# Where a layer's last projection and its early row maxima run: four transformer layers in fp32 on one core

## The chip, the core and the metric

One Trainium2 chip, one of its cores. The time is that of one execution of the whole program on the device, in microseconds (us); lower is better. TensorE (PE) multiplies matrices into the eight banks of its accumulator memory, VectorE (DVE) and ScalarE (ACT) read those banks, GpSimd (POOL) works on the other memory, and SyncE (SP) issues the transfers.

## The reference

Four layers, A, B, A, B, each of the form x = x + attention(layernorm(x)). x has 2048 rows of 576 numbers; there are 32 heads of 18.

```python
def _A_ref(x, wqkv, wo):            # every head has its own keys and values
    qkv = (x @ wqkv).reshape(B, S, 3, H, Dh).transpose(2, 0, 3, 1, 4)
    q, k, v = qkv[0], qkv[1], qkv[2]
    p = softmax(einsum("bhqd,bhkd->bhqk", q, k) * Dh ** -0.5)
    return einsum("bhqk,bhkd->bhqd", p, v).transpose(0, 2, 1, 3).reshape(B, S, D) @ wo
# _B_ref is the same, with one head of keys and values that all 32 heads of queries share
x = x + _A_ref(_layernorm(x), A_wqkv, A_wo)
x = x + _B_ref(_layernorm(x), B_wq, B_wk, B_wv, B_wo)
x = x + _A_ref(_layernorm(x), A_wqkv, A_wo)
x = x + _B_ref(_layernorm(x), B_wq, B_wk, B_wv, B_wo)
```

## The kernel before

**Units.** A layer's attention is cut into 64 units: 16 pairs of heads (a = 0 and 1, on the upper and the lower half of TensorE's rows) by 4 blocks of 512 queries. A unit has 32 score matmuls for row maxima (queries on the partitions, 128x512, read by DVE, which reduces each to its maximum), 32 score matmuls for the exponentials (keys on the partitions, 128x512, read by ACT, which writes `pt` or `side`), and the products of exponentials and values (PV), 16 chunks of 256 columns, summed in the bank `oacc`. The maxima of a unit must be known before its exponentials, since they go into the score matmul as two more rows of `big` (by way of DVE's transpose `tr`, the tensor `m_d` and a transfer). So maxima run 14 steps (`LEAD`) ahead, 56 of them before the first unit.

**Order inside a unit.** The order is written by hand: `UNIT` lists 24 entries, each with two letters, one for each a (`e` exponential, `m` maximum, `d` and `t` the two halves of a cheaper way to take two maxima: ACT writes a difference to `side`, DVE then adds it to a score and takes the maximum in one instruction; a star means that one instruction reads two neighbouring banks), and the PV columns that follow the entry. `BANKS` says which of the seven banks of `banks` each entry takes. PV trails by `LAG` = 1152 columns, so that the first unit's entries 1 to 9 have no PV behind them; `oacc` is idle there. The first two units' maxima don't use `d` and `t` (`FIRST_SHARED`): the buffer `side` lies where the transposed input `xx` lies, and is handed out when the projections are through.

**The head of a layer.** Before the units a layer is normalised, transposed and projected: `project(T, t)` is 14 matmuls of 512 columns ("terms" below: high and low parts of the weights `big` by those of the input `xx` or `yx`) into one bank, which ACT and DVE (or, with `filler`, ACT twice and then POOL) split into a high and a low part, stored to `qk_d` and loaded from there into `big` by `load_k` and `load_q`. `project_v_part` is 14 matmuls of 288 columns for the values. Into this work `beat` weaves the 56 maxima, four at a time (one call of `max_pairs`; the calls are numbered 1 to 14 here): `woven(f, left, every)` calls f `left` times, each after `every` terms. In A layers all 14 calls lie in the list `fill` (eight `project_v_part`, then four projections). In B layers five calls lie among the projections of the third block of tokens (T = 2), five among those of the fourth (T = 3), where `project(3, 4)` makes the keys, and four in `fill` (two projections). A call's four maxima take the banks 4, 5, 6 and one of 0 to 3, which the projections take in turn too. In B layers calls 10 and 11 read the keys of the fourth block.

**Queues.** Each engine works strictly in the order of the code. SP waits for each transfer's inputs in order too, so a load behind a store waits for the store's turn.

Of the kernel before, what the change touches and what calls it, by code (L numbers as in the profile page):

```python
# [9 lines left out]
F32 = mybir.dt.float32  # L10
# [9 lines left out]
P = 128  # L20
# [25 lines left out]
STEPS = 8  # L46
LEAD = 14

FREE = 8, 4
NM_AT = 3  # L50
ROW_AT = 5
SUM_AT = 4
# [77 lines left out]
ENDS = ends(UNIT[:CUT_AT])  # L130
MAX_OPS = [max_ops(k[CUT:] + k[:CUT]) for k in KINDS]
PLAIN = [(i // 2 % 4, i // 8 % 2 * 2 + i % 2) for i in range(16)]
FIRST_SHARED = 2


class Engine:
# [78 lines left out]
def tile_kernel(ctx: ExitStack, tc: tile.TileContext, A_x, A_wqkv, A_wo, B_x, B_wq, B_wk, B_wv, B_wo, out):  # L215
# [58 lines left out]


    turns = {"e": [0, 1, 2, 3], "m": [4, 5, 6]}

    def bank(b, name=None):
        return banks[:, b]
# [263 lines left out]
    for layer in range(4):  # L543
# [9 lines left out]


        def project(T, t, filler=False, half=None, terms=TERMS):
            t0 = T * 512
            n = 114 if not is_a and t == 4 else P
            ps = half_done.pop(t) if t in half_done else (etile if filler else mtile)("psq")
            us = slice(0, 2) if half is None else slice(half, half + 1)
            w = wtile(t)  # L560
            for xc, wc in terms:
                pe.matmul(ps[:n].rearrange("p (u t) -> p u t", u=2)[:, us], w[:, wc, :n], xts[T][:, us, xc, :],
                       start=(xc, wc) == TERMS[0], stop=(xc, wc) == (TERMS if half != 0 else TERMS_LO)[-1])
                beat()
            if half == 0:
                half_done[t] = ps
                return
            ev = [ptile("ev", dt=F32R) for _ in range(2)]
            ev_f = [e.bitcast(F32) for e in ev]
            act.activation(ev[0][:n], ps[:n], AF.Copy)  # L570
            r0, r1 = ((64, P) if t == 4 else (0, P)) if is_a else (96, 96 + DH)
            if T < 2 and t in (range(4, 9) if is_a else (4,)):
                key_diff(T, t, ps, r0, r1)
            if filler:
                raw = ptile("raw")
                act.activation(raw[:n], ps[:n], AF.Copy)
                nc.gpsimd.tensor_tensor(ev[1][:n], raw[:n], ev_f[0][:n], op=OP.subtract)
            else:
                dve.tensor_tensor(ev[1][:n], ps[:n], ev_f[0][:n], op=OP.subtract)
            if not is_a and t == 4:  # L580
                vt = ptile("t")
                act.activation(vt[64:82], ps[64:82], AF.Copy)
                store(ev_f, 96, 96 + DH, D, t0)
                store(ev_f, 0, 64, 512, t0)
                vts.append((T, vt))
            elif t == 4:
                store(ev_f, 64, P, D, t0)
                store(ev_f, 0, 64, 512, t0)
            else:
                store(ev_f, 0, P, t * P, t0)  # L590
# [165 lines left out]
            for a in range(2):  # L756
                max_mm(a, functools.partial(bank, b + a), joined)

        kept = []

        def max_pair():
            if is_a and m_done[0] % 4 == 0:
                run_todo(m_done[0] // 4)
            for a in range(2):
                if m_done[0] % 4 < 3:
                    max_mm(a, mtile)
                else:
                    max_mm(a, (lambda name: kept.pop(0)) if kept else etile)
            if not is_a and m_done[0] == 46:
                max_store(0, 0)  # L770
            elif not is_a and m_done[0] == 50:
                max_rows(0, 0)
# [63 lines left out]
        for T in range(4):  # L836
# [6 lines left out]
                ts = (4, 0, 1, 2, 3) if T < 3 else (4, 0, 1)  # L843
            for i, t in enumerate(ts):
                if not is_a and T == 2 and i == 1:
                    woven(max_pairs, 5, 10)
                elif not is_a and T == 3:
                    woven(max_pairs, *((1, 7), (2, 6), (2, 6))[i])
                project(T, t, not is_a and T >= 2)
                if is_a and T == 3 and i == 2:  # L850
                    load_k(0, 0, 1536)
# [63 lines left out]
        def pts_of(p, u, kc):  # L915

            if (p, u, kc) not in pts:
                n_p[0] += 1
                r = n_p[0] // 3 % 3
                if n_p[0] % 3 or (p, u) == (NPAIR - 1, 3) or sided.get(r) in pts:  # L920
                    pts[p, u, kc] = two("pt")
                else:
                    pts[p, u, kc] = side[:, 3 + 2 * r:5 + 2 * r]
                    sided[r] = p, u, kc
# [87 lines left out]
        for p in range(NPAIR):  # L1012
# [8 lines left out]
                for i in range(4 if is_a else 2):  # L1021
                    at(LEAD + 32 * (p - 1) + 1 + 8 * i if p else LEAD + 6 + i, load_part, p + 1, i)
            if is_a or p == 0:
                at(max(LEAD + 32 * (p - 2) + 20, LEAD + 10 * p), load_kd, p)
        for c in range(5):
            at(49 + 4 * c, finish_loads)
            at(48 + 4 * c, load_wsm, c, A_wo if is_a else B_wo, nc.gpsimd, nc.gpsimd, True)
# [15 lines left out]
        at(b - 2, out_t, 0, dve)  # L1043
        at(b - 1, out_rows, 1)
        left = LEAD - m_done[0] // 4
        work = len(TERMS) * sum(288 / 512 if f is project_v_part else 1 for f, _ in fill)
        woven(max_pairs, left, (work - FREE[layer % 2]) / left)
        for f, args in fill[:-1]:
            f(*args)
        kept.extend([etile("psm") for _ in range(weave["left"])])  # L1050
        fill[-1][0](*fill[-1][1])
        assert not weave["left"] and not kept
        halves.clear()
        side = xtile("side", (P, 9, 512), F32)
        late, n_r, n_p, sided = LAG, [0], [0], {}
        for w in range(4 * NPAIR):
            p, u = divmod(w, 4)
            more_m = w < 4 * NPAIR - 2
# [2 lines left out]
            for i, (kinds, cols) in enumerate(table):  # L1061
# [17 lines left out]
                            max_mm(a, take)  # L1079
                skip = min(late, cols)  # L1080
                late -= skip
                pv_cols(cols - skip)
            assert e_next == [16, 16]
        assert not diffs[0] and not diffs[1]
        outs = out_proj(layer == 3)
        for st in range(ns, ns + L_AT + 1):
# [37 lines left out]
```

## Time and profile before

| | |
|---|---|
| median of 3 runs | 5536.77 us (5536.75 to 5538.99) |
| the profiled execution | 5534.68 us, of which its span 5532.5 us |
| PE, DVE, ACT, POOL busy | 99%, 89%, 85%, 26% of the span |
| mean granted clock of TensorE | 0.998 |

The span runs from the first to the last instruction; some 2.2 us lie around it. The first unit of the four layers begins at about 211, 1537, 2967 and 4297 us. Matmuls are pipelined and their ends are modelled, so waits of PE are read from the distances between the starts of its rows.

### The profile page before, as it was taken

How to read it: one execution, taken by the hardware profiler on the slowest of the kernel's cores; microseconds unless marked ns; L12 is line 12 of the kernel's file. 1: busy time of each engine (PE TensorE's matmuls, PEld its weight loads, DVE VectorE, ACT ScalarE, POOL GpSimd, SP SyncE). 2: the span in 40 equal slices, each digit the busy share in tenths (PEclk: the TensorE clock that was granted, in tenths of full speed). 3: DMA queues.
4: the chain of work that ended last, by engine and by line, in shares of the span. 5: the costliest groups of instructions: out<-in, count | busy, mean ns of one | idle time of the engine just before them, and what ended most of it. 6: DMA issues, size and time to landing. Idle time of an engine off the chain costs nothing.

```text
span 5532.5 us, 163956 instructions
## 1 busy us (share of the span) xinstructions
PE 5494.3 (99%) x63772; PEld 3242.2 (59%) x63772; DVE 4936.3 (89%) x9004; ACT 4709.4 (85%) x7780; POOL 1424.3 (26%) x3267
## 2 busy tenths in 40 slices
PE   9999999999999999999999999999999999999999
PEld 8655555555855555555686555555558555555556
DVE  5799999997699999999647999999977999999995
ACT  3599999999289999999625999999992999999995
POOL 3132222223232222222321322222232322222221
PEclk9999999999999999999999999999999999999999
DMA  7321111111421110101253211111114211110102
GB/s 241 110 50 37 41 37 41 38 37 34 130 63 25 24 25 21 25 22 25 62 202 94 51 40 37 41 37 41 35 36 135 55 25 25 25 25 21 25 15 81
DMA packets 295540, 295.34 MB, mean 53 GB/s; under 512 B 151132, under 2 KB 228188, under 8 KB 285040
## 3 DMA queue, kind: packets, MB, share of 16 engines
q1 hardware_dynamic: 294760, 284.85, 18.3%
q8 instruction: 500, 8.19, 0.6%
q14 instruction: 280, 2.29, 0.1%
HBM read 158.77 MB, written 121.95 MB: 51 GB/s over the span
## 4 chain that ended last, share of the span: by engine, by line
PE 96%; DVE 1%; ACT 1%; issue 0%; SPq 0%; DMA 0%; POOL 0%; ACTq 0%; DVEq 0%; POOLq 0%
PE banks L147 58%; PE oacc L147 38%; DVE mx L147 1%; ACT pt L147 0%; ACT side L147 0%; DMA qk_d<-ev 0%; DVE yx L147 0%; DVE xx L147 0%; DVE xh L147 0%; SPq L977 0%; ACT raw L147 0%; ACT ev L147 0%; DVE ev L147 0%; SPq L1000 0%; DVE st L147 0%
## 5 line engine op out<-in xcount | busy, mean ns | idle before, releaser
L147 DVE TENSOR_REDUCE mxd<-banks 128x1 f32<-128x512 f32 (+1 forms) x6200 | 3955.6, 705 | 143.5 <-PE banks L147 112.6
L147 ACT ACTIVATE pt<-banks 128x512 f32<-128x512 f32 (+1 forms) x4248 | 2927.9, 740 | 120.5 <-PE banks L147 83.3
L147 PE MATMUL banks<-big 62*128 62x512 f32 (+1 forms) x15640 | 2784.9, 438 | 13.8 <-DVE mx L147 4.6
L147 PEld LDWEIGHTS banks<-big 62*128 62x128 f32 (+1 forms) x15640 | 1571.9, 184 | 1158.1 <-DVE mxd L147 538.0
L147 ACT ACTIVATE side<-banks 128x512 f32<-128x512 f32 (+1 forms) x2836 | 1907.2, 697 | 66.0 <-PE banks L147 65.6
L147 PE MATMUL oacc<-pt,vbuf 128*19 128x256 f32 (+3 forms) x20496 | 1279.7, 342 | 0.0
L981 POOL TENSOR_TENSOR rl<-lt,mone 128x8 f32<-128x8 f32 x256 | 428.3, 1673 | 1339.9 <-DMA lt<-os 1298.3
L147 PEld LDWEIGHTS oacc<-pt,vbuf 128*19 128x19 f32 x20496 | 450.6, 98 | 505.1 <-issue 329.7
L147 PE MATMUL oacc<-side,vbuf 128*19 128x256 f32 (+3 forms) x10064 | 676.9, 341 | 2.3 <-DVE ocv L147 2.3
L893 POOL TENSOR_TENSOR tree<-mxd 128x16 f32<-128x16 f32 x248 | 53.1, 214 | 1860.3 <-DVE mxd L147 1860.3
L147 DVE CUSTOM_DVE_ANT_0 side<-banks,side 128x512 f32<-128x512 f32 x744 | 499.0, 671 | 1.3 <-PE banks L147 1.0
L147 PE MATMUL oacc<-pt,vy 128*19 128x256 f32 (+3 forms) x8176 | 444.1, 312 | 0.0
L147 PEld LDWEIGHTS oacc<-side,vbuf 128*19 128x19 f32 x10064 | 223.3, 98 | 246.6 <-issue 157.2
L147 ACT ACTIVATE ev<-banks 128x512 fp32r<-128x512 f32 (+1 forms) x112 | 66.9, 598 | 321.6 <-PE banks L147 245.3
L147 PEld LDWEIGHTS oacc<-pt,vy 128*19 128x19 f32 x8176 | 190.5, 98 | 179.7 <-issue 115.3
L147 PE MATMUL banks<-kd,big 54*128 54x512 f32 x744 | 295.2, 397 | 0.0
L147 PE MATMUL banks<-wsm,ot 128*128 128x288 f32 x1792 | 243.7, 296 | 2.1 <-issue 2.1
L147 PEld LDWEIGHTS banks<-wsm,ot 128*128 128x128 f32 x1792 | 238.4, 188 | 6.4 <-issue 5.2
L147 PE MATMUL oacc<-side,vy 128*19 128x256 f32 (+3 forms) x4016 | 240.7, 311 | 0.0
L147 DVE TENSOR_TENSOR ev<-banks,ev 128x512 fp32r<-128x512 f32 (+1 forms) x84 | 57.9, 690 | 171.6 <-ACT ev L147 156.3
L147 PE MATMUL banks<-xx,big 128*128 128x512 f32 (+1 forms) x784 | 195.3, 398 | 4.1 <-ACT raw L147 4.1
L147 PE MATMUL banks<-yx,big 128*128 128x512 f32 (+2 forms) x812 | 193.8, 391 | 4.4 <-DVE yx L147 2.5
(91 smaller groups left out, 2690.4 us busy)
## 6 DMA issues: line engine op xcount, KB each, us to landing
big<-qk_d SPq DMA_DIRECT2D x180, 432.0 KB
qk_d<-ev SPq DMA_DIRECT2D x96, 512.0 KB
qk_d<-ev SPq DMA_DIRECT2D x120, 256.0 KB
rb<-r_d SPq DMA_DIRECT2D x1024, 18.0 KB
o_d<-os SPq DMA_DIRECT2D x1024, 18.0 KB
lt<-os SPq DMA_DIRECT2D x1024, 1.0 KB
o<-o_d SPq DMA_DIRECT2D x64, 256.0 KB
big<-m_d SPq DMA_DIRECT2D x512, 4.0 KB
```

Of the source, the lines that this page charges most:

```text
L147: i = f(*args, **kw)
L893: nc.gpsimd.tensor_tensor(above, mx[:, :, 0:2], mx[:, :, 2:4], op=OP.subtract)
L981: nc.gpsimd.tensor_tensor(rl, lts.pop((p, u)), mone, op=OP.pow)
```

## The change

The last projection of `fill` is taken out of the head. Its 14 terms run in the first unit, 7 behind entry 3 and 7 behind entry 6, into `oacc`, which PV doesn't need yet; ACT reads it out behind the second seven. `side` is handed out only after that, so the third chunk of exponentials goes to an ordinary `pt` buffer, and the third unit's maxima too are taken without `d` and `t` (`FIRST_SHARED` 3). The maxima of the head no longer take banks in turn: each pair goes to banks 3 and 4 or to 5 and 6, by turns, and one DVE instruction reduces both banks; the projections beside them keep banks 0 to 2. The calls come at other distances: in A layers every 7.36 terms' worth in place of 7.93; in B layers six among T = 2 (every 9 terms, before five, every 10), six among T = 3 (before five), two in `fill` (before four). The transfer `load_kd` of the first pair moves half a unit later.

```diff
-FREE = 8, 4
+FREE = 2, 2
-FIRST_SHARED = 2
+FIRST_SHARED = 3
+FIRST_FILL = 7, 7
+    max_banks = [3, 5]
         def project(T, t, filler=False, half=None, terms=TERMS):
+            for _ in project_terms(T, t, filler, half, terms):
+                beat()
+
+        def project_terms(T, t, filler=False, half=None, terms=TERMS, ps=None):
-            ps = half_done.pop(t) if t in half_done else (etile if filler else mtile)("psq")
+            if ps is None:
+                ps = half_done.pop(t) if t in half_done else (etile if filler else mtile)("psq")
-                beat()
+                yield
         def max_pair():
-            for a in range(2):
-                if m_done[0] % 4 < 3:
-                    max_mm(a, mtile)
-                else:
-                    max_mm(a, (lambda name: kept.pop(0)) if kept else etile)
+            b = max_banks.pop(0)
+            max_banks.append(b)
+            max_two(b)
                 if not is_a and T == 2 and i == 1:
-                    woven(max_pairs, 5, 10)
+                    turns["e"].remove(3)
+                    woven(max_pairs, 6, 9)
                 elif not is_a and T == 3:
-                    woven(max_pairs, *((1, 7), (2, 6), (2, 6))[i])
+                    woven(max_pairs, *((2, 6), (2, 6.5), (2, 6.5))[i])
-                if n_p[0] % 3 or (p, u) == (NPAIR - 1, 3) or sided.get(r) in pts:
+                if n_p[0] % 3 or side is None or (p, u) == (NPAIR - 1, 3) or sided.get(r) in pts:
-                at(max(LEAD + 32 * (p - 2) + 20, LEAD + 10 * p), load_kd, p)
+                at(max(LEAD + 32 * (p - 2) + 20, LEAD + 10 * p, LEAD + 4), load_kd, p)
+        last_terms = project_terms(*fill.pop()[1], ps=oacc)
+        if is_a:
+            turns["e"].remove(3)
         woven(max_pairs, left, (work - FREE[layer % 2]) / left)
-        for f, args in fill[:-1]:
+        for f, args in fill:
             f(*args)
-        kept.extend([etile("psm") for _ in range(weave["left"])])
-        fill[-1][0](*fill[-1][1])
-        side = xtile("side", (P, 9, 512), F32)
+        side, first_fill = None, list(FIRST_FILL)
                 skip = min(late, cols)
                 late -= skip
+                if skip and first_fill:
+                    for _ in range(first_fill.pop(0)):
+                        next(last_terms)
+                    if not first_fill:
+                        assert next(last_terms, True)
+                        side = xtile("side", (P, 9, 512), F32)
                 pv_cols(cols - skip)
```

PE's order at the end of the first layer's head, before: `xx,big` rows are terms, `big` rows with x4 are a call's maxima, the x24 are the first unit's entries 1 to 12 (row 83 is the end of the last projection), `oacc<-pt` is the first PV.

```order
79 L147 MATMUL banks<-xx,big 128x512 x8
80 L147 MATMUL banks<-big 128x512 x4
81 L147 MATMUL banks<-xx,big 128x512 x8
82 L147 MATMUL banks<-big 128x512 x4
83 L147 MATMUL banks<-xx,big 128x512 x7
84 L147 MATMUL banks<-big 128x512 x24
85 L147 MATMUL oacc<-pt,vbuf 19x256 x4
```

The same place of the changed kernel:

```order
79 L148 MATMUL banks<-xx,big 128x512 x7
80 L148 MATMUL banks<-big 128x512 x4
81 L148 MATMUL banks<-xx,big 128x512 x7
82 L148 MATMUL banks<-big 128x512 x4
83 L148 MATMUL banks<-xx,big 128x512 x2
84 L148 MATMUL banks<-big 128x512 x6
85 L148 MATMUL oacc<-xx,big 128x512 x7
86 L148 MATMUL banks<-big 128x512 x6
87 L148 MATMUL oacc<-xx,big 128x512 x7
88 L148 MATMUL banks<-big 128x512 x12
89 L148 MATMUL oacc<-pt,vbuf 19x256 x4
```

Two terms, not seven, lie between call 14 (row 82) and the first unit, and the last projection stands in two sevens between its entries.

PE's order in a B layer's fourth block, before: row 2465 is the second half of the key projection `project(3, 4)` (114 columns of weights), the `big` rows are calls 7, 8, 9 and 10, `ident,t` turns the values.

```order
2465 L147 MATMUL banks<-xx,big 114x512 x7
2466 L147 MATMUL banks<-xx,big 128x512 x6
2467 L147 MATMUL banks<-big 128x512 x4
2468 L147 MATMUL banks<-xx,big 128x512 x6
2469 L147 MATMUL banks<-big 128x512 x4
2470 L147 MATMUL banks<-xx,big 128x512 x2
2471 L147 MATMUL banks<-ident,t 128x18 x4
2472 L147 MATMUL banks<-xx,big 128x512 x6
2473 L147 MATMUL banks<-big 128x512 x4
2474 L147 MATMUL banks<-xx,big 128x512 x6
2475 L147 MATMUL banks<-big 128x512 x4
2476 L147 MATMUL banks<-xx,big 128x512 x8
```

And in the changed kernel, where the `big` rows are calls 8, 9 and 10:

```order
2466 L148 MATMUL banks<-xx,big 114x512 x6
2467 L148 MATMUL banks<-big 128x512 x4
2468 L148 MATMUL banks<-xx,big 114x512 x2
2469 L148 MATMUL banks<-xx,big 128x512 x7
2470 L148 MATMUL banks<-big 128x512 x4
2471 L148 MATMUL banks<-xx,big 128x512 x6
2472 L148 MATMUL banks<-big 128x512 x4
2473 L148 MATMUL banks<-xx,big 128x512
2474 L148 MATMUL banks<-ident,t 128x18 x4
```

Between the end of the key projection and call 10, the first that reads those keys, stood 26 terms, three calls and the turning of the values; now there are 13 terms and one call.

## Rows read from the trace of the kernel before

**Rows 1.** Page, part 4: the chain that ended last, by engine, then by line.
```profile
PE 96%; DVE 1%; ACT 1%; issue 0%; SPq 0%; DMA 0%; POOL 0%; ACTq 0%; DVEq 0%; POOLq 0%
```

**Rows 2.** Timeline, DVE: start, us, instruction; one transpose a unit, each in a unit's middle.
```profile
220.40 0.20 DVE L147 STREAM_TRANSPOSE tr<-hl 128x32 f32<-128x32 f32 x1
238.75 0.20 DVE L147 STREAM_TRANSPOSE tr<-hl 128x32 f32<-128x32 f32 x1
...
1548.14 0.20 DVE L147 STREAM_TRANSPOSE tr<-hl 128x32 f32<-128x32 f32 x1
...
2978.94 0.20 DVE L147 STREAM_TRANSPOSE tr<-hl 128x32 f32<-128x32 f32 x1
2998.42 0.20 DVE L147 STREAM_TRANSPOSE tr<-hl 128x32 f32<-128x32 f32 x1
...
4306.70 0.20 DVE L147 STREAM_TRANSPOSE tr<-hl 128x32 f32<-128x32 f32 x1
```

**Rows 3.** Timeline, PE, first layer's head and first unit; brackets: idle before, who ended it.
```profile
168.27 2.13 PE L147 MATMUL banks<-wsm,xx 128*128 128x288 f32 x15
...
171.00 2.14 PE L147 MATMUL banks<-wsm,xx 128*128 128x288 f32 x14
173.07 0.73 PE L147 MATMUL banks<-big 62*128 62x512 f32 x4
173.73 2.11 PE L147 MATMUL banks<-wsm,xx 128*128 128x288 f32 x14
...
207.49 0.73 PE L147 MATMUL banks<-big 62*128 62x512 f32 x4
...
211.28 0.97 PE L147 MATMUL banks<-big 64*128 64x512 f32 x6 [0.80 <-ACT raw L147]
...
216.98 0.85 PE L147 MATMUL oacc<-pt,vbuf 128*19 128x256 f32 x16
```

**Rows 4.** Windows of all engines: PE, PEld, DVE, ACT, POOL busy, granted clock, DMA.
```profile
2969.50:2976.00 6.50, 6.09 (x33) 3.38 (x33) 5.92 (x10) 4.96 (x8) 1.76 (x8) 0.50 0.57 163
1540.00:1545.50 5.50, 5.50 (x31) 2.82 (x32) 4.66 (x8) 4.08 (x8) 1.76 (x8) 0.50 0.54 153
```

**Rows 5.** Timeline, PE: first exponentials of the second and third layers.
```profile
1537.22 0.97 PE L147 MATMUL banks<-big 64*128 64x512 f32 x6 [0.81 <-ACT raw L147]
...
2967.43 1.78 PE L147 MATMUL banks<-big 62*128 62x512 f32 x9 [1.24 <-ACT raw L147]
```

**Rows 6.** Lines with shapes kept apart, DVE: instructions, busy us, mean ns, idle before.
```profile
L147 DVE TENSOR_REDUCE mxd<-banks 128x1 f32<-128x512 f32 x5952 | 3695.8, 683 | 143.5 <-PE banks L147 112.6
...
L147 DVE TENSOR_REDUCE mxd<-banks 128x2 f32<-128x1024 f32 x248 | 301.7, 1217 | 0.0
```

**Rows 7.** Timeline, DVE: the four maxima of the call at 173.07.
```profile
173.60 2.48 DVE L147 TENSOR_REDUCE mx<-banks 128x1 f32<-128x512 f32 x4 [0.24 <-PE banks L147]
```

**Rows 8.** Timeline, PE, fourth layer: key projection's end, calls 7 and 10, first unit.
```profile
4270.85 3.24 PE L147 MATMUL banks<-xx,big 128*114 128x512 f32 x13
4274.02 0.73 PE L147 MATMUL banks<-big 62*128 62x512 f32 x4
...
4282.69 0.73 PE L147 MATMUL banks<-big 62*128 62x512 f32 x4
...
4297.02 1.78 PE L147 MATMUL banks<-big 62*128 62x512 f32 x9 [1.24 <-ACT raw L147]
...
4303.23 0.85 PE L147 MATMUL oacc<-pt,vbuf 128*19 128x256 f32 x16
```

**Rows 9.** Timeline, SP, fourth layer: the keys' load (x2), a store, the load behind it.
```profile
4276.93 1.23 SPq L670 DMA_DIRECT2D big<-qk_d  x2
...
4280.20 0.35 SPq L625 DMA_DIRECT2D qk_d<-ev  x1
4283.21 0.65 SPq L670 DMA_DIRECT2D big<-qk_d  x2
```

**Rows 10.** Timeline, ACT, first layer: the first of the last projection's two readings.
```profile
210.14 0.60 ACT L147 ACTIVATE ev<-banks 128x512 fp32r<-128x512 f32 x1 [4.51 <-PE banks L147]
```

More of the change, by code (lines that the diff above doesn't have):

```diff
@@ L757, in max_two @@
                 max_mm(a, functools.partial(bank, b + a), joined)
-        kept = []
         def max_pair():
@@ L1045, in tile_kernel @@
         left = LEAD - m_done[0] // 4
+        last_terms = project_terms(*fill.pop()[1], ps=oacc)
         work = len(TERMS) * sum(288 / 512 if f is project_v_part else 1 for f, _ in fill)
+        if is_a:
+            turns["e"].remove(3)
         woven(max_pairs, left, (work - FREE[layer % 2]) / left)
-        for f, args in fill[:-1]:
+        for f, args in fill:
             f(*args)
-        kept.extend([etile("psm") for _ in range(weave["left"])])
-        fill[-1][0](*fill[-1][1])
-        assert not weave["left"] and not kept
-        halves.clear()
-        side = xtile("side", (P, 9, 512), F32)
+        assert not weave["left"]
         late, n_r, n_p, sided = LAG, [0], [0], {}
+        side, first_fill = None, list(FIRST_FILL)
         for w in range(4 * NPAIR):
@@ L1081, in tile_kernel @@
                 late -= skip
+                if skip and first_fill:
[4 more added lines that the diff above has]
+                        side = xtile("side", (P, 9, 512), F32)
                 pv_cols(cols - skip)
             assert e_next == [16, 16]
+        turns["e"].append(3)
         assert not diffs[0] and not diffs[1]
```

## The prediction

> **What bounds the kernel now.** I read the page's chain first: 96% of it is TensorE's work [rows 1], so the kernel is as long as PE's matmuls and PE's pauses. Next, DVE's one transpose a unit shows the pace: 18.35 us a unit [rows 2]. The order of instructions is the same from the third unit of each layer on; only four heads and the units behind them can change. I therefore went to PE's timeline there, with what DVE, ACT and SP do beside it.
>
> The prices come from two places. In the first layer 14 value terms take 2.07 us (171.00 to 173.07) and a call's four maxima 0.66 (to 173.73) [rows 3]; in the fourth 13 terms of 512 columns take 3.17 [rows 8]. A call is two pairs of matmuls, each pair side by side on the halves of the array. With t for a 512-column term or pair and s for each change between whole and half rows, 13t + s = 3.17 and 2t + s = 0.66: t = 0.228, s = 0.20, and a value term is 0.133. The calls of the first layer's head come 2.7 apart, which is 14 x 0.133 + 0.20 + 0.66: PE is full there. It pauses at the head's end, where it waits for ACT's reading, and in the first unit, where 12 pairs (2.7 us) take 5.70, from 211.28 to 216.98 [rows 3]. There DVE and ACT set the pace, PE has some 2.8 us to spare, and it is there that the change puts 3.2 us of terms.
>
> **The clock.** In the second and third layers the granted clock is 0.50, the lower of its two levels (1.2 of 2.4 GHz), for a stretch of the first unit [rows 4]; before the fall PE had only short pauses, 0.81 and 1.24 us [rows 5]. From the first exponential to the unit's middle the four layers take 9.12, 10.92, 11.51 and 9.68 us [rows 2, 3, 5, 8]; the third layer's next unit takes 19.48 instead of 18.35. So the low clock costs 1.2 in the second layer (against the fourth, a B layer too) and 2.4 + 1.1 in the third: 4.8 in all. With 14 more matmuls in just this stretch I expect no fall there: **-4.8** (0 if the falls stay).
>
> **A heads.** One reduction of two banks shows 1217 ns, a single one 683 [rows 6], and four singles take 2.48, so one each 0.60 [rows 7]; the double one then costs 0.60 + 0.53 = 1.13, a call 2.26 of DVE in place of 2.39. But fixed banks make a call wait for the last. DVE starts 0.53 behind PE (173.07 to 173.60) [rows 3, 7]; its second reduction starts at 1.66 and ends at 2.88, and only then can PE write banks 5 and 6. Spaced by work alone, calls 13 value terms apart come every 2.59; with T and T' two calls, the pair on 5 and 6 starts no sooner than T + 2.94, and the spacing settles at half of 2.94 + 0.43 plus the terms between: 2.65, and 2.59 for 7 terms (2.46 by work). Thirteen spacings (seven of 13 value terms, the rest 7, 8 or 11 terms mixed) sum to 34.3, so call 14 starts at 168.27 + 2.07 + 34.3 = 204.6; now it is 207.49. Behind it stand two terms, then entry 1, which takes the bank of the third projection: PE waits for ACT's two readings, 1.14 from the start of the first to PE's restart (210.14 to 211.28) [rows 3, 10]. That puts the first exponential at 204.6 + 2.6 = 207.2, 4.1 sooner.
>
> **The first unit.** Twelve pairs, 14 terms and four more changes of rows are 2.7 + 3.2 + 0.8 = 6.7 us of PE. On top, ACT reads the projection twice (1.1) in front of entry 7's exponential; entries 10 and 12 want banks that ACT frees late, and PE waits about 1.4, and 0.3 at entry 2 for bank 6. The first PV comes 8.5 behind the first exponential, not 5.7. Bounds: 5.7, if the terms fit in the gaps, to 5.7 + 3.2 + 0.8 + 1.1 = 10.8; I take 8.5, for PE's order is fixed and the gaps are not where the terms stand. First PV: 207.2 + 8.5 = 215.7 against 216.98: **-1.2 in each A layer**.
>
> **B heads.** Here DVE has the transposed input's low parts to make as well, and one more call stands before T = 3. Worked call by call with the same rule, the waits for banks 3 to 6 grow by about 1.7 us up to the key projection's end, and two more calls precede it (2 x 0.86): it ends at 4275.8; now at 4270.85 + 7 x 0.228 = 4272.4 [rows 8]. The keys then go through ACT, POOL and two transfers. Their loads leave SP from 4276.93 to 4278.16; a store in that queue holds its reader until 2.66 after its issue (4280.55 to 4283.21) [rows 9], so they land near 4281, and at the latest at 4282.69, where call 10 reads them without a pause [rows 8]. From projection to landed keys it is thus 5.8 to 10.3; I take 8.9, near the store's. Now 10.3 us of other work lie between. After the change there are 13 terms, one call and two changes, 4.0: **PE waits 4.9 for the keys** (1.8 to 6.3), behind it stand all the terms and calls 11 to 14, and DVE runs dry. Call 10 starts at 4284.7, 2.0 later than now. From there 29 terms, five calls and their changes, the values' turning, bank waits of 1.8 and ACT's reading make 14.4 to the first exponential (4299.1, now 4297.02), and 8.5 to the first PV: 4307.6 against 4303.23, **+4.4 in each B layer**.
>
> **Third unit's maxima, SP and POOL.** Three `d`/`t` pairs become six plain maxima: DVE pays three more of 0.60, 1.8 a layer, and ACT loses three readings. A unit's 24 single maxima, one double and three pairs (no less than three singles) hold DVE 17.3 of 18.35, so two units have 2 us of room: 0 to 1.8 a layer, taken as **+0.3**, x4. The moved projection's store now stands behind the next pair's first load, whose reader is more than half a unit away; `load_kd` and the later `side` are read a unit later: nothing. The row of maxima that the first exponential needs is ready sooner by as much as the calls are.
>
> **Sum.** -4.8 - 2 x 1.2 + 2 x 4.4 + 4 x 0.3 = +2.8 us. The profiled execution had 5534.68 (span 5532.5 and 2.2 around it) and becomes 5537.5; the median of the runs is 2.1 above it, so the forecast is **5539**.
>
> **Rivals.** *The clock falls in the B heads.* The wait for the keys is four times the longest pause ahead of a fall now. If the clock falls there, PE's work between call 10 and the first exponential (29 terms and five calls, 11 us) runs in part at half speed. By the falls seen a fall costs 1.2 to 3.5; if the low level lasts the whole way, 11. At 6 a layer the sum is +14.8: 5551, slower. It decides above 4 a layer. The Trainium skill speaks for it ("TensorE: Matmul & The Clock Gate", section "HAM oscillation — how this bites in real kernels"): a pause of PE on a transfer throttles the clock, so that the next matmuls start slow. The trace agrees that pauses bring a fall, but its falls followed pauses of about 1 us, so no row here shows what a long one does. *The terms do fit.* If the first unit's start takes 6.5 in place of 8.5 (DVE and ACT had work in hand when the terms begin), that is -2.0 x 4; if the keys land 5.8 behind the projection, the wait is 1.8, another -3.1 x 2. Sum: 2.8 - 8 - 6.2 = -11.4: 5525, faster. For it speaks that PE idles half of this stretch today; against it that the keys' path has five steps in strict order. *The low clock stays in the middle layers*: +4.8, 5544, no change that shows.
>
> **How the numbers follow.** 0.2% is 11 us, about what a measurement of this kernel can tell from no change. The forecast with its own bounds (5530 to 5547; the third rival in it) has 0.59, the faster rival 0.22, the slower 0.19. The range, 5523 to 5551, reaches to both, and leaves out only their far ends: the terms for nothing and a low clock over a whole head.
>
> **What will show it.** PE's rows in A heads: calls 2.6 apart, first PV 8 to 9 us behind the first exponential. In B heads: at call 10 a pause of some 5 us that the profile puts down to the transfer `big<-qk_d`, first PV some 23 us behind call 10 (now 20.5). In the windows: granted clock 1.00 at the first units, and whether it is 0.50 behind call 10. The prediction is wrong if the keys' pause is under 2 us, or if the first unit costs no more than now.

## The result and the profile after

The changed kernel takes 5546.25 us, the median of 20 runs (5543.62 to 5550.42); the kernel before, run beside it, takes 5535.85 (20 runs). The ratio is 1.0019 [1.0013, 1.0026]: 10.4 us slower, 7 above the forecast and inside its range. One execution each of two versions below took far longer (19179 us for e6_a_shared2, the profiled one; 6346 us for e8_order_shared2) and is left out. The profiled execution's span grew by 9.7, from 5532.5 to 5542.2 us. On the page almost nothing moves; the chain that ended last is again PE's.

```profile
PE 96%; DVE 1%; ACT 1%; issue 1%; DMA 0%; POOL 0%; SPq 0%; POOLq 0%; ACTq 0%; DVEq 0%
```

DVE's timeline after, one transpose a unit, answers to [rows 2]: the first three of the first layer, then the second and third of the other layers.

```profile
197.10 0.20 DVE L148 STREAM_TRANSPOSE tr<-hl 128x32 f32<-128x32 f32 x1
...
220.23 0.20 DVE L148 STREAM_TRANSPOSE tr<-hl 128x32 f32<-128x32 f32 x1
239.48 0.20 DVE L148 STREAM_TRANSPOSE tr<-hl 128x32 f32<-128x32 f32 x1
...
1553.45 0.20 DVE L148 STREAM_TRANSPOSE tr<-hl 128x32 f32<-128x32 f32 x1
1572.68 0.20 DVE L148 STREAM_TRANSPOSE tr<-hl 128x32 f32<-128x32 f32 x1
...
2982.00 0.20 DVE L148 STREAM_TRANSPOSE tr<-hl 128x32 f32<-128x32 f32 x1
3001.24 0.20 DVE L148 STREAM_TRANSPOSE tr<-hl 128x32 f32<-128x32 f32 x1
...
4316.26 0.20 DVE L148 STREAM_TRANSPOSE tr<-hl 128x32 f32<-128x32 f32 x1
4335.51 0.20 DVE L148 STREAM_TRANSPOSE tr<-hl 128x32 f32<-128x32 f32 x1
```

In every layer the second and third stand 19.23 to 19.25 apart, where the pace is 18.35; the third layer's 19.48 of before had another cause, the clock. In the first layer the second transpose is where it was, in the fourth it is 9.6 later.

PE's timeline after, end of the first layer's head and first unit, answers to [rows 3]:

```profile
204.94 0.74 PE L148 MATMUL banks<-big 62*128 62x512 f32 x4
...
207.57 1.04 PE L148 MATMUL banks<-big 62*128 62x512 f32 x4 [0.32 <-ACT raw L148]
208.55 1.91 PE L148 MATMUL oacc<-xx,big 128*128 128x512 f32 x7
...
211.28 1.88 PE L148 MATMUL oacc<-xx,big 128*128 128x512 f32 x7
...
214.88 1.47 PE L148 MATMUL banks<-big 62*128 62x512 f32 x5 [0.57 <-ACT pt L148]
216.28 0.85 PE L148 MATMUL oacc<-pt,vbuf 128*19 128x256 f32 x16
```

The start of call 14 (204.94, forecast 204.6), of the first unit (207.57, forecast 207.2) and of PV (216.28, forecast 215.7) are 0.3 to 0.6 behind those of the working. In the pause of 0.57 behind the second seven terms PE waits for a bank whose exponential ACT takes only after it has read the projection.

PE's timeline after in the fourth layer answers to [rows 8]: the key projection's last 2 terms and 7 of the next projection in one row (x9; the keys' part ends near 4277.9), 6 more terms, call 10 (4285.76 and 4286.60), the first unit (4303.56) and PV.

```profile
4277.46 2.34 PE L148 MATMUL banks<-xx,big 128*114 128x512 f32 x9
...
4280.40 1.65 PE L148 MATMUL banks<-xx,big 128*128 128x512 f32 x6
4285.76 0.47 PE L148 MATMUL banks<-big 62*128 62x512 f32 x1 [3.71 <-DMA big<-qk_d]
4286.60 0.81 PE L148 MATMUL banks<-big 62*128 62x512 f32 x3 [0.38 <-DMA big<-qk_d]
...
4288.61 3.36 PE L148 MATMUL banks<-xx,big 128*128 128x512 f32 x7
...
4303.56 1.10 PE L148 MATMUL banks<-big 62*128 62x512 f32 x6 [1.17 <-ACT raw L148]
...
4312.31 0.85 PE L148 MATMUL oacc<-pt,vbuf 128*19 128x256 f32 x16
```

PE waits 3.71 and 0.38 us for the keys, and behind the wait 7 terms take 3.36 us where 9 took 2.34 ahead of it. The windows say why. Their columns are those of [rows 4]: the first row is the first layer's stretch between its second and third transposes, the second lies behind the second layer's key wait, the third is the third layer's first unit, the fourth lies behind the fourth layer's key wait.

```profile
220.23:239.48 19.25, 18.93 (x234) 9.91 (x232) 18.85 (x33) 16.92 (x28) 2.14 (x9) 1.00 0.50 138
1522.30:1529.10 6.80, 5.93 (x16) 3.72 (x16) 2.50 (x3) 1.08 (x2) 1.28 (x1) 0.50 0.26 99
2970.00:2976.00 6.00, 6.00 (x30) 3.64 (x27) 3.85 (x7) 3.59 (x7) 0.65 (x1) 1.00 0.62 200
4287.10:4293.90 6.80, 6.80 (x19) 4.21 (x19) 3.67 (x5) 1.08 (x2) 1.28 (x1) 0.50 0.32 121
```

The low clock has left the first units and stands behind the key waits. In the first row DVE is busy 18.85 of 19.25 us. The same stretch before had 17.77 of 18.35:

```profile
220.40:238.75 18.35, 18.35 (x237) 9.97 (x235) 17.77 (x33) 17.66 (x30) 2.12 (x9) 1.00 0.46 119
```

### The profile page after: what moved, and what is told of

Its sections match the earlier page's. It is cut to its first block, busy times and chain, and to the rows that moved or that the text cites. A ratio compares the mean times of both kernels' runs of the same rounds, so it can differ in the third digit from the quotient of the medians.

```text
span 5542.2 us, 163762 instructions
## 1 busy us (share of the span) xinstructions
PE 5498.4 (99%) x63772; PEld 3242.1 (58%) x63772; DVE 4935.9 (89%) x8892; ACT 4704.6 (85%) x7768; POOL 1429.9 (26%) x3267
## 4 chain that ended last, share of the span: by engine, by line
PE 96%; DVE 1%; ACT 1%; issue 1%; DMA 0%; POOL 0%; SPq 0%; POOLq 0%; ACTq 0%; DVEq 0%
PE banks L148 58%; PE oacc L148 38%; DVE mx L148 1%; ACT pt L148 0%; ACT side L148 0%; DVE yx L148 0%; DVE xh L148 0%; DVE xx L148 0%; ACT ev L148 0%; DMA big<-qk_d 0%; DVE st L148 0%; DMA qk_d<-ev 0%; DMA raw<-in_A_wqkv_dram 0%; DVE ev L148 0%; ACT raw L148 0%
## 5 line engine op out<-in xcount | busy, mean ns | idle before, releaser
L148 DVE TENSOR_REDUCE mxd<-banks 128x1 f32<-128x512 f32 (+1 forms) x6100 | 3891.6, 705 | 135.6 <-PE banks L148 102.0
L148 DVE TENSOR_REDUCE mx<-banks 128x1 f32<-128x512 f32 (+1 forms) x268 | 228.9, 915 | 41.6 <-PE banks L148 40.6
```

What stands on the lines that cost most here:

```text
L148: i = f(*args, **kw)
```

## The experiments

The kernels are compared by their medians against the kernel before on the same chip, and by one distance of the profile that leaves the scatter of the other stretches out: up to the second transpose of a layer, in A layers from the first value term of the head's end (168.27 before), in B layers from the first term of the second projection over the third block (1487.33 and 4247.12 before). "Low" says in which layers' head or first unit the granted clock was 0.50.

| kernel | median, before beside it | ratio | layer 1 | 2 | 3 | 4 | low |
|---|---|---|---|---|---|---|---|
| before | 5535.85 | | 52.1 | 60.8 | 54.5 | 59.6 | 2, 3 |
| changed | 5546.25, 5535.85 | 1.0019 [1.0013, 1.0026] | 51.7 | 67.0 | 51.7 | 67.1 | 2, 4 |
| e1_keys | 5540.70, 5534.03 | 1.0011 [1.0002, 1.0020] | 51.8 | 65.9 | 51.8 | 63.5 | 2, 4 |
| e2_dummy | 5540.38, 5534.03 | 1.0012 [1.0003, 1.0020] | 51.7 | 64.9 | 51.8 | 64.7 | none |
| e3_shared2 | 5539.69, 5534.03 | 1.0010 [1.0001, 1.0019] | 51.2 | 66.4 | 51.1 | 66.3 | 2, 4 |
| e4_a_only | 5530.39, 5534.03 | 0.9994 [0.9985, 1.0003] | 51.8 | 60.4 | 51.7 | 59.0 | 2 |
| e5_order | 5541.89, 5535.98 | 1.0012 [1.0003, 1.0021] | 51.8 | 65.3 | 51.7 | 65.5 | 2, 4 |
| e6_a_shared2 | 5528.31, 5535.98 | 0.9986 [0.9977, 0.9995] | - | - | - | - | - |
| e7_pairs_only | 5531.48, 5535.98 | 0.9991 [0.9982, 1.0000] | 52.8 | 60.8 | 52.3 | 60.8 | 1, 2, 3, 4 |
| e8_order_shared2 | 5538.96, 5535.98 | 1.0005 [0.9996, 1.0014] | 51.2 | 64.7 | 51.1 | 65.0 | 2, 4 |
| e9_before_spare | 5531.34, 5536.49 | 0.9992 [0.9984, 1.0001] | 52.7 | 59.7 | 52.8 | 59.7 | none |
| e10_a_spare | 5527.55, 5536.49 | 0.9986 [0.9977, 0.9995] | 51.2 | 59.7 | 51.2 | 59.6 | none |
| e11_order_spare | 5534.07, 5536.49 | 0.9997 [0.9988, 1.0006] | 51.2 | 62.6 | 51.2 | 62.8 | none |

Two cautions go with the table. An interval reaches 4 to 5 us to either side, so differences of 3 to 5 us between two of these kernels don't stand by the runs alone; they are given as the ratios have them and held against the distances. And each profile is one execution: where the clock falls varies from one execution to the next. The 33 executions of the kernel before that were run beside e1 to e4 have a mean granted clock of 0.997 (3 of them), 0.998 (20) or 0.999 (10), and take 5538.8, 5534.8 and 5531.8 us on average. All 11 of e2 have 1.000 and lie within 1.6 us.

The theory after the result: the B heads lose by the wait for the keys and by the low clock behind it, and all layers by the third unit's plain maxima. The rivals: the moved terms or the fixed banks cost this time, or it is waited out elsewhere once the key wait is gone.

### e1_keys: the key projection earlier, call 10 later

```diff
-woven(max_pairs, *((2, 6), (2, 6.5), (2, 6.5))[i])
+woven(max_pairs, *((1, 7), (2, 6.5), (2, 6.5))[i])
```

> Changed kernel, but in the B layers' heads one call fewer stands ahead of the key projection's end (weave (1, 7) in place of (2, 6)), so that two calls and 21 terms stand between that projection and call 10, and three calls are left for the fill. Theory (the pause for the keys, and the low clock behind it, are what the B heads lost): the work between the two is 4.0 + 0.9 + 7 x 0.228 + 0.7 = 7.2 us against the 8.4 that the keys take, so the pause falls from 4.4 to about 1 us, the granted clock stays at 1.00 there, and the first PV of each B layer comes 5 to 7 us sooner than in the changed kernel: 5546 becomes 5534. Rival (the row of maxima, which now is finished later against the first exponential, or DVE's joint reductions take the pause's place): the pause at call 10 vanishes too, but PE then waits ahead of the first exponential and the first PV gains under 2 us a B layer: 5543.

The pause at call 10 went as the theory has it, to 0.35 and 0.17 us in the fourth layer. By the ratios the kernel gained some 4 us where the theory had 12; the B layers' distances fell by 1.1 and 3.6. PE's timeline, fourth layer, call 10 and the last call but one:

```profile
4285.32 0.47 PE L148 MATMUL banks<-big 62*128 62x512 f32 x1 [0.35 <-DMA big<-qk_d]
4285.96 0.73 PE L148 MATMUL banks<-big 62*128 62x512 f32 x3 [0.17 <-DMA big<-qk_d]
...
4292.73 0.51 PE L148 MATMUL banks<-big 62*128 62x512 f32 x2
4294.97 0.79 PE L148 MATMUL banks<-big 62*128 62x512 f32 x2 [1.74 <-DVE mx L148]
4295.69 2.07 PE L148 MATMUL banks<-xx,big 128*128 128x512 f32 x4
```

DVE's timeline at the same place:

```profile
4286.49 5.99 DVE L148 TENSOR_REDUCE mx<-banks 128x2 f32<-128x1024 f32 x5 [2.29 <-PE banks L148]
4293.60 0.21 DVE L148 STREAM_TRANSPOSE tr<-hl 128x32 f32<-128x32 f32 x1 [1.12 <-POOL hl L906]
```

The three calls of the fill stand only 4 terms apart now. DVE is behind with its reductions, and its transpose waits 1.12 for POOL's final maxima with the next reductions queued behind it; PE then waits 1.74 for their bank, and the granted clock falls there: 0.50 over 4295.0 to 4298.4 in the fourth layer and over 1533.6 to 1543.8 in the second. So the theory was right on the wait and wrong on the clock; part of the rival came true.

### e2_dummy: the wait stays, PE is kept at work in it

```diff
+            if not is_a and m_done[0] == 36:
+                for _ in range(18):
+                    pe.matmul(oacc, wtile(4)[:, 0, :], xts[3][:, :, 0, :], start=True, stop=True)
```

> Changed kernel with 18 more matmuls of 512 columns into the accumulators' bank just ahead of call 10 in each B layer (their result is never read; the output stays the reference's): 18 x 0.228 = 4.1 us of PE in what was a pause of 4.4. Theory (the pause costs twice, by itself and by the low clock that follows it): call 10 starts where it does in the changed kernel, the granted clock is 1.00 behind it, and from call 10 to the first exponential it takes 14.8 in place of 17.8 us: -3 in each B layer, 5540. Rival (what stands behind call 10 is paced by DVE's reductions or the row of maxima, and the low clock costs nothing): the clock is 1.00 and the 17.8 us stay: 5546.

PE's timeline, fourth layer, the spare matmuls, call 10, the first unit; then the windows from call 10 to the first unit in both B layers:

```profile
4279.81 4.24 PE L148 MATMUL oacc<-xx,big 128*128 128x512 f32 x18
4283.98 1.20 PE L148 MATMUL banks<-big 62*128 62x512 f32 x4
...
4299.09 1.11 PE L148 MATMUL banks<-big 62*128 62x512 f32 x6 [1.17 <-ACT raw L148]
```

```profile
1523.50:1538.60 15.10, 12.62 (x53) 7.19 (x53) 11.57 (x12) 3.26 (x6) 4.30 (x10) 1.00 0.33 120
4284.00:4299.10 15.10, 12.67 (x55) 7.26 (x54) 11.61 (x12) 3.26 (x6) 4.30 (x10) 1.00 0.33 120
```

From call 10 to the first unit it takes 15.1 us, against 17.8 in the changed kernel's fourth layer (4285.76 to 4303.56) and 17.6 in its second; the clock is 1.00 throughout, although the later pauses of 1.05 and 1.17 are still there. The theory holds: the low clock behind the key wait costs 2.5 to 2.7 in each B layer; the wait itself is still there, filled. By the ratios the kernel gained 4 (forecast 6).

### e3_shared2: `d` and `t` back in the third unit's maxima

```diff
-FIRST_SHARED = 3
+FIRST_SHARED = 2
-                at(max(LEAD + 32 * (p - 2) + 20, LEAD + 10 * p, LEAD + 4), load_kd, p)
+                at(max(LEAD + 32 * (p - 2) + 20, LEAD + 10 * p), load_kd, p)
```

> Changed kernel with FIRST_SHARED back at 2 and the difference rows' load back at its earlier block: the third unit's maxima are made with d and t again, from the first unit's fifteenth entry on, when the side places exist. Theory (the +0.9 us by which the first unit to the second grew in all four layers is DVE's, three more plain reductions): DVE's transposes of the first two units stand 18.35 apart again, -0.9 a layer, 5542.6. Rival (the 0.9 comes from the moved terms' debt that the unit carries on): the distance stays 19.25, 5546.

DVE's timeline, first layer, and the windows between its second and third transpose:

```profile
198.58 0.20 DVE L148 STREAM_TRANSPOSE tr<-hl 128x32 f32<-128x32 f32 x1
...
221.16 0.20 DVE L148 STREAM_TRANSPOSE tr<-hl 128x32 f32<-128x32 f32 x1
239.50 0.20 DVE L148 STREAM_TRANSPOSE tr<-hl 128x32 f32<-128x32 f32 x1
```

```profile
221.17:239.51 18.34, 18.34 (x237) 9.99 (x235) 17.78 (x34) 17.63 (x30) 2.12 (x9) 1.00 0.46 126
```

The 0.9 is gone in all four layers, and DVE holds 17.78 of 18.34 again. The stretch ahead of it shrank too, from 23.13 (197.10 to 220.23) to 22.58 in the first layer and by 0.5 to 0.6 in the others, since the third unit's maxima begin in the first unit. Together 1.45 a layer, 5.8 in all; by the ratios the runs gained 5. The cause is as the theory says, its price was set too low.

### e4_a_only and e6_a_shared2: the A layers alone

The B layers get the code of before (banks in turn, their weaves, the last projection in the fill, `side` at once); e6 has `FIRST_SHARED` 2 in the A layers too.

```diff
-FIRST_SHARED = 3
+FIRST_SHARED = 3, 2
+            if is_a:
                 b = max_banks.pop(0)
...
+        if is_a:
             last_terms = project_terms(*fill.pop()[1], ps=oacc)
+            work -= len(TERMS)
```

> The change in the two A layers alone; the B layers' heads keep the layout of before (etile and mtile maxima, last projection in the fill, side places at once, FIRST_SHARED 2). Theory (the A heads gained, the B heads lost): against before the first PV comes 0.9 sooner in the first layer and 2.3 in the third, both with 0.9 more in the next unit, the low clock in the third layer's first unit is gone (-3.5 with its second unit), in the second layer it stays; in the B heads nothing changes: some 3 us faster than before, 5533, and 13 faster than the change. Rival (the A heads only shift work, and what is gained there is waited out by the keys, the rows or the next layer): as before, 5536.

3.6 under before, as forecast. The third layer's stretch is 2.8 shorter, with the clock at 1.00 there; the first layer's is 0.4 shorter, and the next distance 0.9 longer; the B layers are 0.4 and 0.6 shorter; up to the third transpose that is 3.6 in all. The interval of the ratio takes in 1, so the runs alone don't settle it.

```diff
-FIRST_SHARED = 3, 2
+FIRST_SHARED = 2, 2
-                at(max(LEAD + 32 * (p - 2) + 20, LEAD + 10 * p, LEAD + 4 * is_a), load_kd, p)
+                at(max(LEAD + 32 * (p - 2) + 20, LEAD + 10 * p), load_kd, p)
```

> The change in the A layers alone, with FIRST_SHARED 2 in them as well (the side places exist from entry 7 on, the third unit's d and t start at entry 15). Theory (the later side places alone cost 1.45 us a layer: 0.55 in the first unit, 0.9 up to the second): 2.9 us less than the version with FIRST_SHARED 3 in the A layers, some 6.5 under before. Rival (in the A layers the first unit has room for the three plain maxima): as that version, some 3.5 under before.

7.7 under before, and its interval stays below 1; by the ratios it is 4 under e4 (forecast 2.9). No rows of this version are read; e10_a_spare has the same A layers.

### e7_pairs_only: the fixed bank pairs alone

Against the kernel before:

```diff
-                if m_done[0] % 4 < 3:
-                    max_mm(a, mtile)
-                else:
-                    max_mm(a, (lambda name: kept.pop(0)) if kept else etile)
+            b = max_banks.pop(0)
+            max_banks.append(b)
+            max_two(b)
...
+            turns["e"].remove(3)
```

The last line stands in both kinds of layer and keeps the projections to banks 0 to 2, as in the changed kernel.

> Kernel before with the fixed bank pairs alone: the maxima ahead of the units go to banks 3 and 4 or 5 and 6 and are reduced two at a time; the last projection stays in the fill, side places, FIRST_SHARED, FREE and the weaves stay. Theory (joint reductions alone are worth little: the heads are paced by PE and by ACT's readings, and a call now waits for the one before it): A heads 0 to 2 us shorter, B heads 0 to 2 longer, the low clock in the second and third layer's first unit stays, since PE's pauses ahead of it stay: within 3 us of before. Rival (the pairs were what brought the gain in the A heads and the vanished falls): 4 us or more under before, and granted clock 1.00 in the first units.

4.5 under before, the interval reaching 1.0000. Neither forecast fits. No head is shorter by more than the third layer's 2.2, and the clock is low in all four first units, in the first layer's for the first time:

```profile
214.70:221.50 6.80, 6.80 (x45) 3.55 (x49) 5.07 (x9) 4.76 (x8) 1.77 (x8) 0.50 0.34 98
```

The first layer, which had no fall before, is 0.7 longer. But this profile is the slowest of the version's 11 executions (5533.07). Grouped by mean granted clock (0.997, 0.998, 0.999) they take 5532.4, 5531.4 and 5528.1 us on average, those of the kernel before beside them 5538.7, 5536.1 and 5532.9: at a like clock the pairs are worth some 5 us, and what they bring is not the clock. Part of it shows in the A layers' heads. In the first, the first unit starts 41.3 behind the first value term, where it started 43.0 behind it (168.27 and 211.28 in [rows 3]):

```profile
169.56 2.13 PE L147 MATMUL banks<-wsm,xx 128*128 128x288 f32 x15
...
210.90 1.78 PE L147 MATMUL banks<-big 62*128 62x512 f32 x9 [1.23 <-ACT raw L147]
```

In the third layer it is the same 1.7 sooner; in the B layers it is no sooner. So the fixed pairs aren't what the changed kernel loses by. What they are worth with the clock held was not run.

### e5_order and e8_order_shared2: the keys read later

In the B layers the second unit's maxima over the first two blocks come first, so that calls 11 and 12 are the first to need the fourth block's keys; e8 has `FIRST_SHARED` 2 as well.

```diff
-        m_first = [] if is_a else ([(0, i // 2, i % 2) for i in range(8)] + [(1, i // 2, i % 2) for i in range(4)] +
-                                   [(0, i, 2) for i in range(4)] + [(1, i // 2, i % 2) for i in range(4, 6)] +
-                                   [(0, i, 3) for i in range(4)] + [(1, i // 2, i % 2) for i in range(6, 8)] +
+        m_first = [] if is_a else ([(0, i // 2, i % 2) for i in range(8)] + [(1, i // 2, i % 2) for i in range(8)] +
+                                   [(0, i, 2) for i in range(4)] + [(0, i, 3) for i in range(4)] +
-            if not is_a and m_done[0] == 46:
+            if not is_a and m_done[0] == 50:
...
-            elif not is_a and m_done[0] == 50:
+            elif not is_a and m_done[0] == 54:
```

> Changed kernel with one list reordered in the B layers: the calls that read the fourth block's keys are 11 and 12 instead of 10, 11 and a part of those behind (the second unit's maxima over the first two blocks come first, those over its third block wait until calls 13 and 14); the row of maxima is stored and loaded one call later. The weave, and with it where each call stands, is the changed kernel's. Theory (the pause for the keys and the low clock behind it): between the key projection's end and call 11 lie 28 terms and two calls, over 8.4 us, so there is no pause, no low clock, and from the key projection's end to the first exponential it takes 9.6 of terms, 5.2 of calls and some 4 of small waits, 18.8 in place of 25.7: -6.9 in each B layer, so some 3 us under before in place of 10 over. Rival (the row of maxima, 8.4 us from its last maxima to its landing, now ends last): the pause goes, but PE waits ahead of the first exponential; from the key projection's end it takes 21 to 23, and the kernel stays at or above before.

By the ratio 4 under the changed kernel, 6 above before. The key projection ends at 4277.5 and the first unit starts at 4297.73: 20.2, where the theory had 18.8, the rival 21 to 23 and the changed kernel 25.7. Then PE's timeline goes on so, in e5's fourth layer:

```profile
4297.73 0.64 PE L148 MATMUL banks<-big 62*128 62x512 f32 x1 [1.18 <-ACT raw L148]
4299.42 1.61 PE L148 MATMUL banks<-big 64*128 64x512 f32 x5 [1.05 <-DMA big<-m_d]
4300.96 3.36 PE L148 MATMUL oacc<-xx,big 128*128 128x512 f32 x7
...
4310.36 0.85 PE L148 MATMUL oacc<-pt,vbuf 128*19 128x256 f32 x16
```

```profile
4298.00:4304.70 6.70, 5.65 (x15) 3.48 (x16) 2.58 (x4) 1.09 (x2) 1.01 (x1) 0.50 0.60 194
```

The row of maxima lands late (1.05, the rival's wait), and the clock falls here in place of there: the stretch from the first unit's start to PV takes 12.6 instead of 8.7. Of the 5.5 us won ahead of the first unit, 3.9 are lost behind its start.

> Changed kernel with both repairs: the reordered list of the B layers and FIRST_SHARED 2 in all layers. Theory (the two parts are independent): -13.8 and -5.8 against the changed kernel, some 9 us under before. Rival (the two gains overlap, since what the second unit waits for is one and the same debt): no faster than the better of the two alone, some 3 under before.

3 above before, within the interval. Against e5 the ratio falls by 0.0007, some 4 us, and the distances up to the third transpose by 5.6 in all, of the 5.8 that `side` was worth alone. So the two gains add, but the clock's loss is in both.

### e9_before_spare: the clock by itself

Against the kernel before:

```diff
+            if not is_a and m_done[0] == 50:
+                spare_mm(4)
...
+                if w == 0 and i in (0, 2):
+                    spare_mm(4 if i == 0 else 2)
```

`spare_mm(n)` is n matmuls of 512 columns from weights into `oacc`.

> Kernel before with spare matmuls of 512 columns into the accumulators' bank, whose result is never read, in the pauses of the heads' ends: 4 ahead of the first unit's first entry and 2 ahead of its third in every layer, and in the B layers 4 ahead of the second half of call 13 (the output stays the reference's). It measures the clock's term by itself. Theory (the low clock in the second and third layer's first unit comes from these pauses and costs 1.2 and 3.5 us): granted clock 1.00 in all four first units, third layer's first two transposes 18.35 apart in place of 19.48, some 4 under before. Rival (the low clock has another cause, or the spare matmuls take as much time as they give back): the falls stay, or the kernel is within 2 of before.

5 under before, the interval reaching 1.0001. DVE's transposes in the third layer, and the windows of the second and third layers' first units:

```profile
2976.47 0.20 DVE L147 STREAM_TRANSPOSE tr<-hl 128x32 f32<-128x32 f32 x1
2994.82 0.20 DVE L147 STREAM_TRANSPOSE tr<-hl 128x32 f32<-128x32 f32 x1
```

```profile
1537.50:1549.20 11.70, 11.60 (x91) 5.89 (x92) 11.05 (x20) 9.77 (x17) 3.05 (x9) 1.00 0.42 137
2966.70:2976.00 9.30, 8.98 (x68) 4.59 (x68) 8.68 (x15) 7.48 (x12) 3.05 (x9) 1.00 0.52 170
```

The second layer's stretch is 1.1 shorter, now as long as the fourth's. The third layer's is 1.7 shorter, and the next distance is 18.35 in place of 19.48: 2.8 in all. The six spare matmuls themselves cost the first layer, which had no low clock to lose, 0.6. So the falls of before cost 1.2 in the second layer and 3.4 in the third. Nine of this version's 11 executions have a mean granted clock of 1.000, none of the 27 of the kernel before beside them.

### e10_a_spare and e11_order_spare: both together

e10 is e6 with the spare matmuls in its B layers, e11 is e8 with more of them.

```diff
 e10
+            if not is_a and m_done[0] == 50:
+                spare_mm(4)
+                if not is_a and w == 0 and i in (0, 2):
+                    spare_mm(4 if i == 0 else 2)
 e11
+            if not is_a and m_done[0] == 54:
+                spare_mm(4)
+                if not is_a and w == 0 and i in (0, 2):
+                    spare_mm(8 if i == 0 else 0)
```

> The change in the A layers alone with FIRST_SHARED 2, as in the run before, and in the B layers, which keep the layout of before, the spare matmuls of the other version (4, 4 and 2). Theory (A heads without a fall by the moved terms, B heads without one by the spare matmuls): the second layer's fall, 0.5 to 1.2 us, goes too: 8 to 9 under before. Rival (the A layers' gain was the vanished fall alone, and the spare matmuls bring nothing): as the version without them, 7.7 under before, or worse.

8.9 under before; its ratio is that of e6, so the runs can't tell the spare matmuls' share from none. In the profile the A layers are 0.9 and 3.3 shorter than before, the second layer 1.1, and the third layer's next distance 1.1: 6.4 in all, of which 4.6 is the clock. This version beats both kernels.

> Changed kernel with the reordered list and FIRST_SHARED 2, and in the B layers 4 spare matmuls ahead of the second half of call 14 and 8 ahead of the first unit, in the pauses for DVE's reductions, for ACT's reading and for the row of maxima. Theory (this version lost in the B layers' first units, by the low clock alone, most of what the reordering gained): granted clock 1.00 behind the first exponential, from it to the first PV 8.7 in place of 12.6 us, -3.4 in each B layer against the version without them: some 4 under before. Rival (the B heads stay slower for the row of maxima and the moved terms, whatever the clock): under 2 a layer, no better than before.

PE's timeline, fourth layer: the spare matmuls, the first exponentials, PV.

```profile
4291.40 1.99 PE L148 MATMUL oacc<-big 128*128 128x512 f32 x8
4293.32 0.50 PE L148 MATMUL banks<-big 62*128 62x512 f32 x1
4294.45 0.94 PE L148 MATMUL banks<-big 64*128 64x512 f32 x5 [0.64 <-DMA big<-m_d]
...
4303.06 0.85 PE L148 MATMUL oacc<-pt,vbuf 128*19 128x256 f32 x16
```

From 4293.32 to PV it takes 9.7 in place of 12.6, and the wait for the row stays. Against e8 the ratio falls by 0.0008: 4.4 of the 6.8 us. With the order of the keys, `side` and the clock all mended, the B heads are still 3.0 us longer than those of before at full clock (62.6 and 62.8 against 59.7). The wait for the row is part of that; what the rest is no run separates. The kernel as a whole can't be told from before.

## Why the forecast came near, and which steps were off

**The clock, -4.8: right.** e9 takes the falls from the kernel before by nothing but work in the pauses, and prices them at 1.2 and 3.4 (forecast 1.2 and 3.5). In the changed kernel the first units have 1.00.

**A heads, -1.2 each: right.** PV comes 47.8 us behind the first value term in both A layers of the changed kernel, against 48.7 in the first layer before: -0.9. The last calls stand 2.5 to 2.7 apart, and from the first exponential to PV it takes 8.7 (forecast 8.5): the moved terms do not fit in the gaps, so the faster rival's first half falls. e7 shows how the 0.9 comes about. With the fixed pairs alone the first unit already starts 1.7 sooner, and in e7's third layer PV comes 47.8 behind the first value term although the clock has fallen by then. The moved terms take 2.3 more out of the head (39.1 against 41.3 to the first unit's start) and cost about as much in the first unit: 8.7 to PV, where a first unit without them takes 6.2 at full clock [rows 8]. So, as far as these profiles show, the gain to PV is the pairs'. The terms' own gain is the clock: in e7 it falls in the A layers' first units, and in no profile of a kernel with the moved terms does it fall there. At the second transpose only 0.4 is left, since half a microsecond goes to the third unit's maxima; with `FIRST_SHARED` 2 it is 1.0 (51.2 against 52.1).

**B heads, +4.4 each: the wait right, what follows it mis-sized.** Counted from the table's first term (1487.33 and 4247.12 before, 1486.42 and 4249.14 after) PV comes 6.7 and 7.1 later. The key projection ends 3.4 later in the fourth layer, as worked out; the wait is 4.1, the sum of its two pieces (forecast 4.9); from the first exponential to PV 8.7. The step that was off is the one from call 10 on, "make 14.4 to the first exponential": it was 17.8. e2 measures why, 15.1 with the clock held. That is the slower rival's mechanism at its place, at 2.5 to 2.7 a layer: below the 4 from which it would have decided, and far from the 6 it was priced at. The 0.7 between 14.4 and 15.1 no run explains. The rule of the Trainium skill ("TensorE: Matmul & The Clock Gate", section "HAM oscillation — how this bites in real kernels"), that a pause of PE on a transfer makes the next matmuls start slow, is what both B layers show behind the waits of 3.87 and 3.71 us.

**Third unit's maxima, +0.3 each: mis-sized, 1.45.** The working gave DVE 17.3 of a unit's 18.35 and so 2 us of room in two units. The windows show 17.77: the room is 1.2 at most, and the extra 1.8 goes nearly all to the path (e3). This is +4.6 of the error.

**The sum.** With these measured in place of the forecast's, +2.8 becomes 2.8 + 2 x 2.6 + 4 x 1.15 = +12.6. Up to the third transpose the four layers' profiles differ by +0.5, +7.1, -3.1 and +8.4, which is +13.0. The rest of the span, the same instructions in the same order, is 3.3 shorter in the changed kernel's profile; it scatters from kernel to kernel (5227.7 to 5232.0 us in the twelve profiles read here). The medians differ by 10.4. No run explains the 2.2 between that and 12.6: by these terms the forecast would have missed by 10, and that it missed by 7 is luck.

So each mechanism of the loss stood in the text with its place. Two prices were low: that of the third unit's maxima lay within its bounds (0 to 1.8), and the low clock behind the wait stood only as a rival, with nothing for it in the sum.

## What to carry to other kernels

A wait on PE is paid twice where the clock falls behind it: price the wait and the slow stretch, and move a wait only to a place where PE has other work. Before a cheap instruction is replaced by a dearer one on an engine that is not the bound, read that engine's busy time from a window of just that unit: at 17.8 of 18.35 "not the bound" means half a microsecond. And take a change apart by layer or stage: here the half in the A layers makes the kernel some 8 us faster once its side cost is gone (of the 5.3 that e10's profile shows in the A layers, 3.4 is the clock), while the half in the B layers, as it was changed, costs more than that.

## What the runs showed of the hardware

The low clock isn't tied to the long wait: e1 and e5 took the 4 us pause away, and the granted clock fell later, behind pauses of 1.1 to 1.7 us among short half-row matmuls (1.74 ahead of 4294.97 in e1; 1.09 ahead of 4295.39 and 1.18 ahead of 4297.73 in e5). Where spare matmuls stood in the pauses (e2, e9, e10, e11) no head and no first unit of the profiled executions had 0.50. Nor do like pauses always bring a fall: e2 kept pauses of 1.05 and 1.17 at 1.00, and the kernel before had 1.24 ahead of the third layer's and of the fourth layer's first unit, with a fall in the third alone [rows 4, 5, 8]. Executions of one kernel differ too, as their mean granted clocks show. Which pauses bring a fall is left open.
